# Order of loads, fills and splits at the start of a fused transformer block, and a split in two pieces at its end

## The chip, the cores and the metric

The kernel runs on one core of one Trainium2 chip. The metric is the device time of one execution in microseconds (us). Three runs of the kernel before took 1048.65, 1049.32 and 1049.63 us; their median is 1049.32 us. A core has five engines that run side by side and wait for each other through semaphores: TensorE (PE, matmuls), VectorE (DVE), ScalarE (ACT), GpSimd (POOL) and SyncE (SP), which here only issues DMAs. Each engine takes its instructions in the order in which they stand in its own queue.

## The reference

Input x has 2048 tokens of 640 features. Everything is float32.

```python
xn = layernorm(x)                                   # eps 1e-5
q, k, v = heads(xn @ wqkv)                          # 32 heads of 20
s = q @ k.T * 20 ** -0.5                            # query sees itself and the 255 tokens before it
attn = softmax(where(0 <= qi - ki < 256, s, -1e9)) @ v
mlp = (gelu(xn @ w_gate) * (xn @ w_up)) @ w_down    # 640 -> 1728 -> 640
out = x + attn @ wo + mlp
```

## The kernel before

**Precision.** A float32 operand is cut into an upper part and a lower part: ACT copies it to a tile that the matmul reads at full rate ("high", "hi"), and DVE or POOL subtracts this from the original and keeps the rest ("low", "lo"). A product is then three matmuls: high by high, low by high, high by low. So each operand costs one pass of ACT and one of DVE or POOL before PE can use it.

**Stages.** The tokens are cut into four chunks of 512 (NC = 4), each into four tiles of 128. (1) The front: the tiles are loaded, normalised and transposed, and q, k and v of the first head groups are computed. (2) Attention: a schedule of slots written out by hand interleaves scores, exponentials and sums with the projections that are still to come. (3) The gate and up products of the MLP, lines 948 and 951. (4) The last phase: the products with w_down and wo, over eight blocks of 256 tokens ("p", two to a chunk) and, in each, nine pairs of weight quads and one short step "e". For most steps (all of p of 2 and more, and the later ones of p = 1) seven products of sums stand in place of eight products, as in Strassen's scheme; a step is then 21 matmuls of 320 columns, and its operand is made of seven pieces: three taken from the loaded tile and four sums `s`.

**The first chunk** (`first_chunk`). x tiles 0 to 3 are normalised two at a time: `ln_stats` (DVE), `ln_sqrt` (DVE and ACT), `ln_rstd` (four DVE instructions), `ln_apply` (DVE, line 161: subtract the mean, scale). `turn` transposes five blocks of 128 features with PE (line 178), `high` copies the upper part from PSUM (ACT, line 349), `low` the rest (DVE, line 346), and `part` multiplies half a chunk with the weights of the first q tile (`wr0`, into `dn[0]`) and of the first k tile (`wr5`, into `dn[1]`), line 353. `high_qk` (ACT) and `low_qk` (POOL) split these weights, `load_v` splits the v weights (ACT line 298, POOL line 299) and sets up the v tiles (POOL, lines 309 and 310). `save_qk` stores q and k: ACT, DVE, ACT, POOL, then two DMAs. After it, `proj_v` makes v of the tokens of the chunk before (line 108), with the transposes of the next chunk among them: after 40 of its matmuls in chunk 1 (`VLEAD`).

**Fills.** Rows of the tiles `ks` and `qs` that hold constants are filled by 14 small DMAs on SP from a tile `ones`, which POOL sets (lines 438 and 439); POOL also builds the mask of the sliding window (lines 464 to 469).

**What sets the order.** Inside `tc.manual_schedule(engines=...)` the engines named keep the order of the program; everything else is placed by a scheduler that simulates the engines and fills each queue in the order of its own estimated times. So in the kernel before, where `first_chunk` names PE, ACT, DVE and POOL, SP is ordered by the scheduler, and work that the program writes after `first_chunk` (the v weights, the fills, the mask) is placed between its instructions. In the last phase all five engines keep the order of the program.

**The last phase** (`split_step`, `prepare`, `plan`). Step n computes its matmuls (`terms`), loads the operand of step n + 4 (SP) and splits that of step n + 2. `plan` says which weight quads are prepared at which step: `f` fetches a quad (a DMA issued by ACT), `h` makes its upper part (ACT), `l` its lower part (DVE), `s` sums, `p` single parts; `b` and `t` are the two kinds of quad. Quads pass through three staging buffers, so a fetch waits until the lower part of the quad three fetches earlier is done. `drain` adds the PSUM banks of a finished block to x and stores it.

Of the kernel before, what the change touches and what calls it, by code (L numbers as in the profile page):

```python
# [20 lines left out]
NC = S // C  # L21
# [47 lines left out]
def block_kernel(ctx, tc, x, wqk, wv, wgu, wdo, wdl, out):  # L69
# [63 lines left out]

    def ln_load(t, lp):
        xi = lp.tile([128, D], F32, name="xi", tag="xi", bufs=8)
        nc.sync.dma_start(xi, x[t * 128:(t + 1) * 128, :])
# [25 lines left out]

    def ln_scale(xs, lp, mv=None):
        n = len(xs)
        if mv is None:
            mv = lp.tile([128, n, 2], F32, name="mv4", tag="mv4", bufs=2)
            for i, xi in enumerate(xs):
                ln_stats(xi, mv[:, i, :], lp)
# [161 lines left out]
    def run(*gens):  # L330
        for gen in gens:
            for _ in gen:
                pass
# [7 lines left out]

    def first_chunk(xs, wr0, wr5, lp):
        halves = slice(0, 256), slice(256, 512)
# [4 lines left out]
        def high(k, ps, cs):  # L348
            nc.scalar.activation(xh[:, k, cs], ps, AF.Copy)
# [6 lines left out]
        def high_qk(raw):  # L356
            wh = wp.tile([128, KT, 128], F32R, name="wqh", tag="wqh")
            nc.scalar.activation(wh, raw, AF.Copy)
            return wh
# [5 lines left out]

        with tc.manual_schedule(engines=MANUAL | {mybir.EngineType.Pool}):
            mv = [lp.tile([128, 2, 2], F32, name="mv", tag="mv", bufs=2) for _ in range(2)]
# [12 lines left out]
            high(0, ta[0], halves[0])  # L380
            for k in range(1, 4):
                high(k, ta[k], halves[0])
            wh5 = high_qk(wr5)
            vb = ln_sqrt(mv[1], 2, lp)
            high(4, ta[4], halves[0])
            for k in range(2):
                low(k, ta[k], halves[0])
            rs = ln_rstd(*vb, 2, lp)
# [5 lines left out]
            nc.gpsimd.tensor_copy(one[:, 0:1], xs[3][:, 0:1])  # L394
            w5 = low_qk(wr5, wh5)
            tb = [turn(0, xs[2:4], "o")]
            for k in range(2, KT):
                low(k, ta[k], halves[0])
# [11 lines left out]
            for i, w in enumerate((w0, w5)):  # L410
                if i:
                    part(dn[i], w[1], xh, halves[0])
                part(dn[i], w[1], xh, halves[1])
                part(dn[i], w[0], xl, halves[1], last=True)
                for j in range(4 if i == 0 else 0):
                    ln_stats(xs[4 + j], mv[:, j, :], lp)
                save_qk(5 * i, 0, dn[i])
        return w0, w5, mv

    v0 = []  # L420
    with tc.tile_pool(name="lp", bufs=1, side="right") as lp:
# [11 lines left out]
        xs += [ln_load(t, lp) for t in range(4, 8)]  # L433
        w0, w5, mv1 = first_chunk(xs, wr0, wr5, lp)
        run(prep)
        v0 = v0[0]
        ones = lp.tile([4, 2 * C], BF, name="ones")
        nc.gpsimd.memset(ones, 0.0)
        nc.gpsimd.memset(ones[0:2], 1.0)
        for i in range(NK):  # L440
            for j in (0, 2):
                nc.sync.dma_start(ks[i][SR:64, j:j + 2].rearrange("p j t -> p (j t)"), ones)
        for c in range(1, NC):
            ln_scale(xs[4 * c:4 * c + 4], lp, mv1 if c == 1 else None)
            vs = [proj_v(v0, 4 * c - 4 + i, None if i % 2 else (psm, "mx")) for i in range(4)]
# [7 lines left out]
            else:  # L453
                ln_turn(4 * c, xs[4 * c:4 * c + 4])
            if c + 1 < NC:
                xs += [ln_load(t, lp) for t in range(4 * c + 4, 4 * c + 8)]
            if c == 1:
                for i in range(NQ):
                    for j in (0, 2):
                        nc.sync.dma_start(qs[i][SR + 2:64, j:j + 2].rearrange("p j t -> p (j t)"), ones[2:4])  # L460
# [683 lines left out]
    def split_step(n, between=None, behind=None):  # L1144
# [17 lines left out]
        if between:  # L1162
            between()
        sub(s[:, 0:2], raw[:, 0:1].to_broadcast([128, 2, 128]), raw[:, 1:3])
        sub(s[:, 2], s[:, 1], raw[:, 1])
        sub(s[:, 3], raw[:, 3], s[:, 2], OP.add)
        if behind:
            behind()
        nc.scalar.activation(hi[:, 3:7], s, AF.Copy)  # L1169
        sub(lo[:, 0:3], raw[:, 1:4], hi[:, 0:3].bitcast(F32))  # L1170
# [163 lines left out]
    for j, f in enumerate(range(NFA, NF - 1)):  # L1334
# [50 lines left out]
        if not end:  # L1385
# [118 lines left out]
```

## Time and profile before

| | |
|---|---|
| median of three runs | 1049.32 us |
| the profiled execution | 1047.46 us |
| its span on the core | 1045.7 us |
| PE busy | 1035.9 us, 99% |
| DVE busy | 730.8 us, 70% |
| ACT busy | 514.7 us, 49% |
| POOL busy | 333.6 us, 32% |
| granted clock of PE | 1.00 |

The times inside a profile count from the start of the span. The profiled execution is one more execution beside the three runs; what it takes beyond its span (1.76 us) lies before the first and after the last instruction. A row of the timeline gives start, length, engine, line, operation, output and inputs, shapes, how many instructions are merged into the row, and in brackets how long the engine had been idle and what ended that. Lengths of neighbouring instructions overlap a little on all engines, so the distance between starts says how fast work goes through.

### The profile page before, as it was taken

Reading aid. Unit: us, or ns where it says so; the run is one execution under the profiler, and the core shown is the slowest. Engines: PE = TensorE matmul, PEld = TensorE weight load, DVE = VectorE, ACT = ScalarE, POOL = GpSimd, SP = SyncE. Lnnn points to the kernel's source line nnn. Section 1 sums busy time; section 2 is a strip of 40 time slices with the busy share of each in tenths; the row PEclk is TensorE's granted clock in tenths of the full one; section 3 lists DMA queues with packets and bytes.
Section 4 is the critical chain, followed back from the end, with each engine's and each line's share of the span. In section 5 each row is a group of like instructions: output and inputs, shape, how many; then the busy total and the mean of one; then the engine's idle time right before and its main releaser. Section 6 shows DMA issues by size and latency. Waiting matters only on the chain.

```text
span 1045.7 us, 22718 instructions
## 1 busy us (share of the span) xinstructions
PE 1035.9 (99%) x7997; PEld 826.6 (79%) x7997; DVE 730.8 (70%) x2007; ACT 514.7 (49%) x1088; POOL 333.6 (32%) x503
## 2 busy tenths in 40 slices
PE   8999999999999999999999999999999999999998
PEld 7987666666677766666666888888888999999998
DVE  8745666666665556676663678877655889888887
ACT  4444666765665566655666522223324554333332
POOL 5121767766564458464634111110110000000000
PEclk9999999999999999999999999999999999999999
DMA  5652455545343244453322556677217874433342
GB/s 200 189 151 86 123 173 153 173 154 184 115 125 89 88 129 145 130 154 116 119 71 77 187 194 235 218 257 250 96 58 250 268 242 137 135 128 113 124 135 93
DMA packets 105179, 158.56 MB, mean 152 GB/s; under 512 B 15420, under 2 KB 60092, under 8 KB 105064
## 3 DMA queue, kind: packets, MB, share of 16 engines
q1 hardware_dynamic: 102680, 150.95, 45.0%
q10 hardware_dynamic: 2384, 6.16, 1.8%
q8 instruction: 63, 1.03, 0.4%
q14 instruction: 52, 0.43, 0.1%
HBM read 101.78 MB, written 54.92 MB: 150 GB/s over the span
## 4 chain that ended last, share of the span: by engine, by line
PE 96%; DVE 2%; DMA 1%; ACT 0%; issue 0%; SPq 0%; DVEq 0%
PE ps_d L108 23%; PE ps_g L948 21%; PE ps L1215 21%; PE ps_e L573 9%; PE ps_o L600 8%; PE ps_v L108 7%; PE ps_m L514 5%; PE ps_g L108 1%; PE ps_t L178 1%; PE ps_d L353 1%; DVE ss L1053 0%; DMA qs<-qd 0%; DVE at L1053 0%; DVE xi L161 0%; DMA xi<-x 0%
## 5 line engine op out<-in xcount | busy, mean ns | idle before, releaser
L518 DVE CUSTOM_DVE_ANT_0 junk<-ps_m,mask 128x320 bf16<-128x320 f32 (+2 forms) x512 | 243.1, 475 | 145.0 <-PE ps_m L514 87.0
L575 ACT ACTIVATE P<-ps_e 128x512 f32<-128x512 f32 (+2 forms) x384 | 198.2, 569 | 64.0 <-PE ps_e L573 58.9
L1215 PE MATMUL ps<-wb,at 128*128 128x320 f32 x999 | 156.2, 309 | 0.1
L1215 PEld LDWEIGHTS ps<-wb,at 128*128 128x128 f32 x999 | 148.9, 188 | 0.6 <-issue 0.3
L586 POOL TENSOR_SCALAR_AFFINE_SELECT P<-P 128x512 f32<-128x512 f32 x128 | 83.5, 653 | 153.6 <-ACT P L575 150.6
L573 PE MATMUL ps_e<-qs,ks 124*128 124x128 bf16 (+2 forms) x704 | 117.4, 278 | 0.3 <-ACT ob L604 0.2
L108 PE MATMUL ps_d<-xh,wqh 128*128 128x512 f32 x350 | 107.8, 416 | 0.0
L108 PE MATMUL ps_d<-xl,wqh 128*128 128x512 f32 x350 | 107.5, 415 | 0.0
L108 PE MATMUL ps_d<-xh,wql 128*128 128x512 f32 x350 | 107.2, 414 | 0.0
L1215 PE MATMUL ps<-wt,at 128*128 128x320 f32 x552 | 89.3, 310 | 0.4 <-DVE u L1053 0.4
L573 PEld LDWEIGHTS <-ks 124*128 124x128 bf16 x704 | 49.5, 98 | 47.7 <-issue 33.6
L600 PE MATMUL ps_o<-P,v 128*32 128x384 f32 (+2 forms) x1408 | 84.5, 387 | 0.0
L1215 PEld LDWEIGHTS ps<-wt,at 128*128 128x128 f32 x552 | 82.9, 188 | 0.9 <-DVE u L1053 0.9
L1169 ACT ACTIVATE at<-ss 128x512 fp32r<-128x512 f32 x59 | 37.3, 632 | 90.3 <-DVE ss L1053 90.2
L589 POOL TENSOR_SCALAR_AFFINE_SELECT P<-P 128x512 f32<-128x512 f32 x112 | 72.7, 659 | 24.8 <-ACT P L575 24.8
L101 POOL TENSOR_TENSOR wql<-wr,wqh 128x640 fp32r<-128x640 f32 x11 | 17.6, 1606 | 174.8 <-PE ps_g L948 149.5
L108 PEld LDWEIGHTS ps_d<-xh,wql 128*128 128x128 f32 x350 | 64.2, 189 | 10.4
L108 PEld LDWEIGHTS ps_d<-xl,wqh 128*128 128x128 f32 x350 | 64.2, 189 | 10.4 <-issue 0.2
L600 PEld LDWEIGHTS ps_o<-P,v 128*32 128x32 f32 x1408 | 41.4, 110 | 38.7 <-issue 21.7
L108 PEld LDWEIGHTS ps_d<-xh,wqh 128*128 128x128 f32 x350 | 63.8, 189 | 10.3 <-issue 0.2
L256 POOL TENSOR_TENSOR pt<-r,pt 128x512 bf16<-128x512 f32 x40 | 46.8, 1171 | 62.8 <-ACT pt L255 62.6
L604 ACT ACTIVATE ob<-ps_o 128x512 f32<-128x512 f32 x32 | 19.1, 597 | 88.9 <-PE ps_o L600 77.6
(194 smaller groups left out, 1849.2 us busy)
## 6 DMA issues: line engine op xcount, KB each, us to landing
hr<-hd SPq DMA_DIRECT2D x104, 128.0 KB
hd<-he SPq DMA_DIRECT2D x50, 256.0 KB
wr<-wgu SPq DMA_DIRECT2D x27, 320.0 KB
qs<-qd SPq DMA_DIRECT2D x64, 120.0 KB
ks<-kd SPq DMA_DIRECT2D x64, 120.0 KB
xi<-x SPq DMA_DIRECT2D x16, 320.0 KB
qs<-qd SPq DMA_DIRECT2D x64, 80.0 KB
ks<-kd SPq DMA_DIRECT2D x64, 80.0 KB
```

Source lines behind the costliest of these rows:

```text
L108: nc.tensor.matmul(ps, a(k), b(k), start=n == 0, stop=n == 3 * nk - 1)
L256: nc.gpsimd.tensor_tensor(out=pt[:, l, :], in0=r, in1=pt[:, 1, :], op=OP.subtract)
L514: nc.tensor.matmul(ps[64 * h:64 * h + 64, lo:hi], q[rows, j, q0:q0 + 64], keys, start=True, stop=True, tile_position=(64 * r, 64 * h))
L518: nc.vector.tensor_tensor_reduce(out=junk[:, 0:n], in0=ps[:, 0:n], in1=mask[:, 320 - n:320], scale=1.0, scalar=NEG, op0=OP.add, op1=OP.max ...
L573: nc.tensor.matmul(ps[:, col:col + n], k[0:QROWS, j, kc:kc + 128], q[0:QROWS, j, q0:q0 + n], start=True, stop=True)
L575: nc.scalar.activation(pt[:, j, lo:hi], ps[:, lo:hi], AF.Exp, scale=SCALE)
L586: nc.gpsimd.affine_select(out=a, in_=a, pattern=[[0, 4], [1, 128]], compare_op=OP.is_ge, fill=0.0, base=0, channel_multiplier=-1)
L589: nc.gpsimd.affine_select(out=a, in_=a, pattern=[[0, 4], [-1, 128]], compare_op=OP.is_ge, fill=0.0, base=-1, channel_multiplier=1)
L600: nc.tensor.matmul(o[32 * j:32 * j + 32, q0:q0 + n], v[:, w0_:w0_ + 32], pt[:, j, col:col + n], start=i == 0, stop=i == len(todo) - 1, ski ...
L948: nc.tensor.matmul(ps, i, j, start=first and n == 0, stop=n == len(work) - 1, skip_group_check=True)
L1169: nc.scalar.activation(hi[:, 3:7], s, AF.Copy)
L1215: nc.tensor.matmul(ps[bank][:, 0:HD], *work[bank][j], start=bank not in begun, stop=final[p, bank] == n and j == len(work[bank]) - 1, skip ...
```

## The change

What it does, in the order of the program:

- `ln_load` can take a tile `behind`: POOL then copies one column of that tile into the new x tile first, so that the load (which overwrites it) can't start before `behind` is there.
- `first_chunk` also keeps SP in the order of the program. All five upper parts of the first half come before the upper part of `wr5`; the square root of the second pair moves between them; one lower part instead of two stands ahead of the second pair's normalisation, and the other four behind it. The split of the v weights (`prep`) runs inside, behind that of `wr5`.
- Tiles 4 to 7 are normalised inside `first_chunk`, between the save of q and the save of k, and the loads of tiles 8 to 11 are issued there, behind tile 4's normalisation.
- The setting of `ones`, the 14 fills and the mask move behind the arrival of tile 11, into chunk 1 of the loop. The loads of tiles 12 to 15 wait until tile 8 is normalised.
- In `split_step` the upper parts of the four sums are made in two instructions of two sums, the first as soon as its sums exist.
- In `plan` three upper parts move ahead of a fetch in ACT's order.

```diff
-    def ln_load(t, lp):
+    def ln_load(t, lp, behind=None):
         xi = lp.tile([128, D], F32, name="xi", tag="xi", bufs=8)
+        if behind is not None:
+            nc.gpsimd.tensor_copy(xi[:, 0:1], behind[:, 0:1])
         nc.sync.dma_start(xi, x[t * 128:(t + 1) * 128, :])
...
-        with tc.manual_schedule(engines=MANUAL | {mybir.EngineType.Pool}):
+        with tc.manual_schedule(engines=MANUAL_OUT | MANUAL | {mybir.EngineType.Pool}):
...
             high(0, ta[0], halves[0])
-            for k in range(1, 4):
+            for k in range(1, KT):
                 high(k, ta[k], halves[0])
+            vb = ln_sqrt(mv[1], 2, lp)
             wh5 = high_qk(wr5)
-            vb = ln_sqrt(mv[1], 2, lp)
-            high(4, ta[4], halves[0])
-            for k in range(2):
-                low(k, ta[k], halves[0])
+            low(0, ta[0], halves[0])
             rs = ln_rstd(*vb, 2, lp)
...
             w5 = low_qk(wr5, wh5)
+            run(prep)
             tb = [turn(0, xs[2:4], "o")]
-            for k in range(2, KT):
+            for k in range(1, KT):
                 low(k, ta[k], halves[0])
...
                 for j in range(4 if i == 0 else 0):
                     ln_stats(xs[4 + j], mv[:, j, :], lp)
+                if i == 0:
+                    vb = ln_sqrt(mv, 4, lp)
                 save_qk(5 * i, 0, dn[i])
-        return w0, w5, mv
+                if i == 0:
+                    rs = ln_rstd(*vb, 4, lp)
+                    for j in range(4):
+                        ln_apply(xs[4 + j], mv[:, j, :], rs[:, j:j + 1])
+                    xs += [ln_load(t, lp, xs[4]) for t in range(8, 12)]
+        return w0, w5
...
-        w0, w5, mv1 = first_chunk(xs, wr0, wr5, lp)
-        run(prep)
+        w0, w5 = first_chunk(xs, wr0, wr5, lp, prep)
         v0 = v0[0]
         ones = lp.tile([4, 2 * C], BF, name="ones")
-        nc.gpsimd.memset(ones, 0.0)
-        nc.gpsimd.memset(ones[0:2], 1.0)
-        for i in range(NK):
-            for j in (0, 2):
-                nc.sync.dma_start(ks[i][SR:64, j:j + 2].rearrange("p j t -> p (j t)"), ones)
         for c in range(1, NC):
-            ln_scale(xs[4 * c:4 * c + 4], lp, mv1 if c == 1 else None)
+            if c > 1:
+                ln_scale(xs[4 * c:4 * c + 4], lp)
...
-            if c + 1 < NC:
-                xs += [ln_load(t, lp) for t in range(4 * c + 4, 4 * c + 8)]
+            if c == 2:
+                xs += [ln_load(t, lp, xs[8]) for t in range(12, 16)]
             if c == 1:
+                nc.gpsimd.tensor_copy(ones[:, 0:1], xs[11][0:4, 0:1])
+                nc.gpsimd.tensor_copy(mask[:, 0:1], xs[11][:, 0:1])
+                nc.gpsimd.memset(ones, 0.0)
+                nc.gpsimd.memset(ones[0:2], 1.0)
+                for i in range(NK):
+                    for j in (0, 2):
+                        nc.sync.dma_start(ks[i][SR:64, j:j + 2].rearrange("p j t -> p (j t)"), ones)
                 for i in range(NQ):
...
         sub(s[:, 0:2], raw[:, 0:1].to_broadcast([128, 2, 128]), raw[:, 1:3])
+        nc.scalar.activation(hi[:, 3:5], s[:, 0:2], AF.Copy)
         sub(s[:, 2], s[:, 1], raw[:, 1])
         sub(s[:, 3], raw[:, 3], s[:, 2], OP.add)
         if behind:
             behind()
-        nc.scalar.activation(hi[:, 3:7], s, AF.Copy)
+        nc.scalar.activation(hi[:, 5:7], s[:, 2:4], AF.Copy)
         sub(lo[:, 0:3], raw[:, 1:4], hi[:, 0:3].bitcast(F32))
         sub(lo[:, 3:7], s, hi[:, 3:7].bitcast(F32))
...
-            7: "ft6 ft8 hb8 lb8", 8: "ft7 ht6 lt6", 9: "ft0 ht8", 10: "lt8 ht7 lt7", 11: "ft1 ft2 ht0 lt0",
+            7: "ft6 hb8 ft8 lb8", 8: "ht6 ft7 lt6", 9: "ht8 ft0", 10: "lt8 ht7 lt7", 11: "ft1 ft2 ht0 lt0",
```

More of the change, by code (lines that the diff above doesn't have):

```diff
@@ L161, in ln_apply, with ln_scale @@
         nc.vector.tensor_scalar(xi, xi, mv[:, 0:1], rs, op0=OP.subtract, op1=OP.mult)
-    def ln_scale(xs, lp, mv=None):
+    def ln_scale(xs, lp):
         n = len(xs)
[L165 to L168, printed above, removed]
+        mv = lp.tile([128, n, 2], F32, name="mv4", tag="mv4", bufs=2)
+        for i, xi in enumerate(xs):
+            ln_stats(xi, mv[:, i, :], lp)
         rs = ln_rstd(*ln_sqrt(mv, n, lp), n, lp)
@@ L340, in block_kernel, with first_chunk @@
         nc.gpsimd.memset(nm, 0.0)
-    def first_chunk(xs, wr0, wr5, lp):
+    def first_chunk(xs, wr0, wr5, lp, prep):
         halves = slice(0, 256), slice(256, 512)
```

## The prediction, made before the changed kernel ran

> **What bounds the kernel now.** I read the page first: busy shares and the chain that ended last.
>
> ```profile
> span 1045.7 us, 22718 instructions
> PE 1035.9 (99%) x7997; PEld 826.6 (79%) x7997; DVE 730.8 (70%) x2007; ACT 514.7 (49%) x1088; POOL 333.6 (32%) x503
> PE 96%; DVE 2%; DMA 1%; ACT 0%; issue 0%; SPq 0%; DVEq 0%
> ```
>
> PE is the bound: 96% of the chain, and 9.8 us of the span in which it does nothing. The change removes no matmul. So it can win only idle PE time, and the question is where that lies. Second view: busy time by stretches (columns: from:to, length, then busy time of PE, weight loads, DVE, ACT, POOL, then granted clock, DMA share, GB/s).
>
> ```profile
> 8.00:10.00 2.00, 1.87 (x14) 1.55 (x13) 1.97 (x6) 1.36 (x5) 1.63 (x2) 1.00 0.99 401
> 10.00:12.00 2.00, 1.31 (x10) 1.11 (x10) 1.79 (x10) 1.46 (x5) 2.00 (x12) 1.00 1.03 408
> 12.00:14.00 2.00, 1.06 (x8) 0.66 (x7) 2.00 (x3) 1.38 (x4) 2.00 (x3) 1.00 0.63 245
> 30.00:62.00 32.00, 32.00 (x197) 29.51 (x196) 21.55 (x52) 13.61 (x44) 6.29 (x8) 1.00 0.52 159
> 804.00:837.00 33.00, 32.93 (x225) 32.67 (x223) 28.38 (x38) 19.44 (x25) 0.00 (x0) 1.00 0.85 284
> 880.00:900.00 20.00, 19.58 (x132) 19.08 (x131) 18.00 (x43) 9.23 (x20) 0.00 (x0) 1.00 0.37 118
> 900.00:1040.00 140.00, 140.00 (x955) 139.92 (x955) 121.41 (x282) 51.67 (x99) 0.00 (x0) 1.00 0.40 128
> 1040.00:1046.00 6.00, 2.36 (x17) 2.10 (x15) 2.00 (x5) 0.00 (x0) 0.00 (x0) 0.94 0.22 82
> ```
>
> From 8 to 14 us PE idles 0.13 + 0.69 + 0.94 = 1.76 us; the changed order of the first chunk lies there. From 880 to 900 it idles 0.42 us, where the split in two pieces works. It is full from 30 to 62 us, and in the last 140 us before the tail; the 3.64 us after 1040 are the last sums and stores, which nothing here touches. What is left lies ahead of 8 us, also untouched, and in scattered waits. The clock is full throughout the work, so it plays no part.
>
> **The first chunk.** Third view, the timeline of all engines.
>
> ```profile
> 7.08 1.14 DVE L161 TENSOR_SCALAR xi<-xi,mv,rs 128x640 f32<-128x640 f32 x2
> ...
> 8.37 0.18 POOL L375 COPY one<-xi 128x1 f32<-128x1 f32 x1 [6.51 <-DVE xi L161]
> ...
> 9.71 0.76 ACT L358 ACTIVATE wqh<-wr 128x640 fp32r<-128x640 f32 x1
> ...
> 10.34 0.32 ACT L149 ACTIVATE sq<-mv,one 128x2 f32<-128x2 f32 x1
> 10.37 0.75 DVE L346 TENSOR_TENSOR xl<-ps_t,xh 128x256 fp32r<-128x256 f32 x2
> ...
> 10.53 0.40 ACT L349 ACTIVATE xh<-ps_t 128x256 fp32r<-128x256 f32 x1
> ...
> 10.98 0.39 PE L353 MATMUL ps_d<-xh,wqh 128*128 128x256 f32 x1 [0.69 <-ACT xh L349]
> 11.03 0.15 DVE L154 RECIPROCAL rs<-sq 128x2 f32<-128x2 f32 x1
> ...
> 11.81 1.96 DVE L161 TENSOR_SCALAR xi<-xi,mv,rs 128x640 f32<-128x640 f32 x2
> 11.82 0.94 POOL L439 MEMSET ones<- 2x1024 bf16 x1
> ...
> 13.69 2.73 DVE L346 TENSOR_TENSOR xl<-ps_t,xh 128x256 fp32r<-128x256 f32 x8
> ...
> 13.82 1.20 PE L178 MATMUL ps_t<-ident,xi 128*128 128x128 f32 x9 [0.32 <-DVE xi L161]
> ...
> 14.78 1.44 PE L353 MATMUL ps_d<-xl,wqh 128*128 128x256 f32 x10
> ```
>
> *Upper parts first.* The fifth product waits 0.69 us for `high(4)`, which stands behind `wh5` (0.76 us) and the root. Changed, it starts in the place of `wh5`, 9.71, ends at 10.11, and PE goes on at about 10.17 instead of 10.98. `wh5` moves behind the root, to 10.53, and ends at 11.29; its five products are still 0.45 us earlier than before. But the gain stops there: next come the transposes of tiles 2 and 3, and these wait for DVE. So DVE's chain prices this stage.
>
> *One `low` instead of two ahead of the normalisation.* Eight take 2.73 us, so one is 0.34 us. The root is there at 10.66; the reciprocal goes from 11.03 to about 10.70, the normalisation from 11.81 to 11.48.
>
> *Fills held back.* The two normalisations took 1.96 us at 11.81, beside POOL's setting of `ones`, and 1.14 us at 7.08, with POOL empty. Changed, POOL waits for tile 3 there (its one-column copy stands ahead of the weight split, and `ones`, mask and v weights come later), so I take 1.14. DVE is through at 12.62 instead of 13.77: 0.33 + 0.82 = 1.15 us.
>
> *What is late next.* Four `low` now follow, and the transposes of blocks 1 to 4 use the PSUM banks that they free. The third of the four starts at 12.54 + 2 x 0.34 = 13.22 and ends near 13.62; then the last two transposes (nine took 0.96 to the next start, so 0.22) let the products start at 13.88 instead of 14.78. **Gain 0.90 us**, of the 1.15 and the 1.76. The ends for this part are 0 (all taken back below) and 1.76; the chain just worked out is nearer the middle, and I keep it.
>
> *Is it taken back in the same chunk?* These are the next meeting points.
>
> ```profile
> 20.35 0.64 DVE L270 TENSOR_TENSOR r<-ps_d,pt 128x512 f32<-128x512 f32 x1
> ...
> 21.73 1.17 POOL L256 TENSOR_TENSOR pt<-r,pt 128x512 bf16<-128x512 f32 x1 [1.80 <-ACT pt L255]
> 21.77 1.48 DVE L161 TENSOR_SCALAR xi<-xi,mv,rs 128x640 f32<-128x640 f32 x1
> ...
> 26.13 2.34 PE L178 MATMUL ps_t<-ident,xi 128*128 128x128 f32 x20
> ```
>
> ACT's root for tiles 4 to 7 now stands ahead of the upper part of q, so `r` starts near 20.6 although the statistics end 0.8 earlier. Its bank is wanted by the second v product, near 21.6: hidden, with 0.3 us left. The four normalisations start near 21.9, one beside POOL's 1.17 us subtraction (1.48 us, as at 21.77), three free (0.57, half of 1.14): done near 25.1, for transposes due at 26.13 - 0.90 = 25.23. Hidden, by little. A second collision costs about 0.8 there and would stall PE by 0.2 to 0.5. The save of k waits behind the four on DVE, and its store in SP behind the four loads; nothing of PE wants it before attention.
>
> **Loads, fills, mask.** The first load in the chain of waits (start, length), then SP's queue and the work that waits for it:
>
> ```profile
> 0.81 2.98 DMA xi<-x
> ```
>
> ```profile
> 12.79 5.16 SPq L442 DMA_DIRECT2D ks<-ones  x8
> 31.57 3.15 SPq L136 DMA_DIRECT2D xi<-x  x4
> 47.33 2.90 SPq L488 DMA_DIRECT2D ks<-kd  x6
> ```
>
> ```profile
> 35.82 2.18 DVE L161 TENSOR_SCALAR xi<-xi,mv,rs 128x640 f32<-128x640 f32 x4
> 38.07 2.35 PE L178 MATMUL ps_t<-ident,xi 128*128 128x128 f32 x20
> 55.88 2.35 PE L178 MATMUL ps_t<-ident,xi 128*128 128x128 f32 x20
> ```
>
> Tiles 8 to 11 go out together near 24.4 to 26.2, and no fill stands between them. PE is full from 30 to 62, so an earlier arrival gains 0; it only feeds slack. The ten added one-column copies on POOL are 0.18 us each (as the one at 8.37), 1.8 us in all, and POOL's 6.29 busy of 32 us hides them. The 14 fills (eight took 5.16 us, so 9.0) now start only after tile 11 and `ones`, by my estimate near 32, and run to about 41; the loads of tiles 12 to 15 (3.15 us) follow, issued by 44 instead of 34.7. From there it takes 10 us: landing 3.0 (first load), statistics 4 (`r` at 20.35 follows four of them, which begin when the eight `low` end at 16.4), scales 0.8 (from 11.03 to 11.81), normalising 2.2. Ready near 54, for transposes due at 55.88 - 0.90 = 55. Cost 0 while that cover holds; the first rival is its loss.
>
> **The last phase.** Groups by shape, then one ACT row and PE's timeline.
>
> ```profile
> L1053 DVE TENSOR_TENSOR at<-ss,at 128x512 fp32r<-128x512 f32 x59 | 40.8, 692 | 11.8 <-ACT at L1169 11.5
> ```
>
> ```profile
> 844.19 0.40 ACT L1150 ACTIVATE he<-hr 128x256 fp32r<-128x256 f32 x1
> ```
>
> ```profile
> 891.45 1.92 PE L1215 MATMUL ps<-wt,at 128*128 128x320 f32 x12
> ...
> 897.61 1.73 PE L1215 MATMUL ps<-wt,at 128*128 128x320 f32 x9
> 899.76 0.70 PE L1215 MATMUL ps<-wt,at 128*128 128x320 f32 x3 [0.42 <-DVE u L1053]
> ```
>
> In 59 steps DVE waits 11.5 us, about 0.2 each, for the one ACT pass over four sums. Split, the second piece covers two sums (0.40 us as 128x256) and ends while DVE makes the lower parts of the loaded pieces: the wait goes. That is worth nothing where PE is full (900 to 1040). It counts at one place: twelve matmuls take 1.92 us at 891.45, and 2.85 us from 897.61 to 899.76 + 0.70, where PE waits for DVE's sums at the change of block: 0.93 us lost. DVE is busy 18.00 of the 20 us around it, so over the four steps ahead it gains about 4 x 0.2 = 0.8 us. Ends 0 and 0.93; I take **0.85 us**, near the upper, since DVE was the late one all along. ACT pays at most one more instruction of 0.40 us a step, 24 us in 59, and it is idle for 88 of the 140 us: hidden. The reorder in `plan` frees ACT and DVE earlier in the 33 us from 804, where PE idles 0.07: 0, and it moves fetches by no more than one upper part.
>
> **The sum.** 0.90 + 0.85 = 1.75 us. The profiled execution took 1047.46 us (span 1045.7), which would become 1045.7; it lay 1.86 us below the median of the runs. Against that median: 1049.32 - 1.75 = **1047.6 us**.
>
> **Rivals.**
> *Slower: tiles 12 to 15 come too late.* The scheduler puts their loads, now behind POOL's copy and 9 us of fills, behind the q and k reloads of attention (last row of SP above, to 50.2). Then they are issued by 53.4 and ready 10 us later, at 63.4, for transposes due at 55: PE stalls 8.4 us, 1056.0. It decides from an issue later than 45. For it: SP's order there is the scheduler's, and 44 is close. Against: the loads stand ahead of the reloads in the program.
>
> *Nothing won: the held POOL work meets the next normalisation.* `ones` (0.94 us for its second half) and the mask now run just after tile 11 lands, near 30 to 34, and the four normalisations of chunk 2 (2.18 us free) follow near 34, ready near 36 for transposes due at 38.07 - 0.90 = 37.2. Each that collides costs up to 0.9 (1.48 against 2.18 / 4); three make 2.7 us, against 1 us of slack: 1.7 lost, 1049.3. For it: the rows at 11.81 and 21.77, both beside POOL. Against: the POOL work should be over by then. [...]
>
> *More won.* All 1.76 us of the first chunk and the 0.93 go, as lower parts and banks keep pace: 1049.32 - 2.69 = 1046.6.
>
> **From cases to numbers.** Within 0.2%, 2.1 us, a measurement of this kernel can't tell a change. Forecast 0.50 (of it 0.08 falls beyond 2.1 us, as the runs spread by half a us), more won 0.24, nothing won 0.16, slower 0.10. Faster 0.08 + 0.24 = 0.32; same 0.42 + 0.16 = 0.58; slower 0.10. The range runs from just below "more won", 1046.3, to 1049.9, above "nothing won"; it leaves out the slow rival.
>
> **What would show it.** Fifth product near 10.2; the pair of normalisations near 11.5 in 1.1 to 1.2 us with POOL idle; products of the lower parts near 13.9; transposes of chunk 1 near 25.2 without an idle time; DVE's wait for L1169's successors near 0 and no stretched row near 898. Wrong it would be by PE idle ahead of the transposes near 37 or 55.

## The result, and the profile after

| | before | after |
|---|---|---|
| median (22 runs of each, the same chip) | 1048.86 us | 1051.36 us |
| lowest and highest | 1047.44 and 1050.83 | 1049.62 and 1054.67 |
| ratio after to before, 95% interval | | 1.0025 [1.0017, 1.0034] |
| span of the profiled execution | 1045.7 us | 1049.0 us |

The change makes the kernel slower by 2.5 us. The forecast was 1047.6 us, no measurable change, with a range from 1046.3 to 1049.9 us. By my estimate about 1 of the 2.5 us goes with a lower mean clock of PE in nine of the 22 runs: the median of all is 1051.36 us, that of the other thirteen 1050.46 (last section).

The page of the changed kernel: its span, the busy shares, and the chain that ended last.

```profile
span 1049.0 us, 22809 instructions
PE 1037.9 (99%) x7997; PEld 827.4 (79%) x7997; DVE 732.3 (70%) x2007; ACT 524.0 (50%) x1147; POOL 336.1 (32%) x513
PE 94%; DVE 3%; DMA 1%; issue 1%; ACT 0%; POOL 0%; SPq 0%; DVEq 0%; ACTq 0%; POOLq 0%
```

The same matmuls, but PE holds 94% of the chain instead of 96%. By stretches (columns as before the change: PE's busy time is the third number):

```profile
10.00:12.00 2.00, 1.90 (x12) 1.46 (x12) 1.82 (x9) 1.84 (x6) 0.01 (x1) 1.00 1.02 406
12.00:14.00 2.00, 1.78 (x13) 1.25 (x12) 2.00 (x7) 2.00 (x7) 1.31 (x2) 1.00 1.01 399
30.00:62.00 32.00, 30.30 (x181) 27.07 (x181) 20.56 (x52) 12.15 (x41) 10.59 (x19) 1.00 0.37 114
880.00:900.00 20.00, 20.00 (x138) 20.00 (x138) 19.15 (x47) 12.18 (x31) 0.00 (x0) 1.00 0.44 132
```

The two stretches that were to win did: 0.32 us idle from 10 to 14 instead of 1.63, none from 880 to 900 instead of 0.42. The stretch that was full, 30 to 62, now has 1.70 us of idle PE.

To see where gains and losses fall, I took the start of each matmul in a trace minus the start of the same matmul in the trace of before. Negative means ahead. The median of five neighbours, in us, at these times of the kernel before (at 60 the matmuls of four kernels stand partly in another order: there it is the value of the next ones in the same order, or a blank); the rows below the first belong to the experiments.

| | 30 | 42 | 60 | 66 | 150 | 160 | 800 | 840 | 905 |
|---|---|---|---|---|---|---|---|---|---|
| the changed kernel | -0.98 | 0.03 | 1.32 | 2.83 | 2.55 | 3.96 | 4.37 | 4.23 | 3.22 |
| e1_last | 0.09 | 0.10 | 0.09 | 0.09 | 0.14 | 0.59 | 1.16 | 0.81 | -0.20 |
| e2_front | -0.78 | 0.45 | 1.74 | 5.16 | 4.87 | 6.42 | 8.02 | 7.67 | 7.64 |
| e3_order | -0.03 | -0.03 | -0.03 | -0.03 | -0.04 | 0.15 | 0.62 | 1.14 | 1.11 |
| e9_hold | 1.72 | 1.71 | 1.71 | 1.71 | 1.76 | 2.28 | 2.78 | 2.46 | 2.45 |
| e11_all | 1.15 | 1.15 | 1.15 | 1.15 | 1.17 | 1.49 | 1.51 | 1.16 | 0.15 |
| e4_x8 | 0.25 | 0.25 | 0.25 | 0.25 | -0.05 | 0.92 | 1.40 | 1.05 | 0.04 |
| e5_x12 | -0.88 | 0.45 | 0.45 | 4.99 | 5.00 | 5.41 | 5.45 | 5.10 | 4.09 |
| e6_both | 0.16 | 0.15 | 0.15 | 0.15 | -0.11 | 0.90 | 2.25 | 2.31 | 1.29 |
| e12_stats | -0.93 | 0.62 | 0.63 | 2.49 | 2.72 | 2.92 | 3.29 | 2.95 | 1.95 |
| e18_best | -0.96 | 0.36 | 0.36 | 0.38 | 0.52 | 1.37 | 1.58 | 1.23 | 0.22 |
| e19_reload | -0.86 | 0.32 | | 7.18 | 7.24 | 7.52 | 7.90 | 7.70 | 6.70 |
| e20_best2 | -0.85 | -0.64 | -0.64 | -0.64 | -0.60 | 0.41 | 0.60 | 0.25 | -0.73 |
| e21_norm2 | -0.87 | -0.87 | 0.42 | 2.76 | 2.49 | 3.17 | 3.50 | 3.47 | 2.47 |
| e22_split | -0.02 | -0.01 | -0.01 | -0.01 | 0.01 | 0.17 | 0.19 | -0.16 | -1.17 |
| e23_plan | 0.04 | 0.04 | 0.04 | 0.04 | 0.04 | -0.11 | 0.51 | 0.15 | 0.63 |

Four of these kernels (e1, e3, e22, e23) are the same as before from 66 to 800 us, and still drift by 0.2 to 1.1 us there from one execution to the next. So only the front (up to 66) and the step from 895 to 905 are read from single traces. By these, the change won 0.98 us in the first chunk, lost 1.0 at chunk 2, 1.3 at chunk 3 and 1.5 at the first scores, and won 1.0 in the last phase; 1.4 more went near 157, which is not settled (below).

The first chunk after the change, from the timeline:

```profile
9.18 1.34 PE L354 MATMUL ps_d<-xh,wqh 128*128 128x256 f32 x5
...
10.43 0.72 ACT L359 ACTIVATE wqh<-wr 128x640 fp32r<-128x640 f32 x1
...
11.42 1.14 DVE L163 TENSOR_SCALAR xi<-xi,mv,rs 128x640 f32<-128x640 f32 x2
...
12.61 1.43 PE L179 MATMUL ps_t<-ident,xi 128*128 128x128 f32 x9 [0.20 <-DVE xi L163]
...
13.80 1.44 PE L354 MATMUL ps_d<-xl,wqh 128*128 128x256 f32 x10
```

The five products run in one piece, the pair of normalisations takes 1.14 us from 11.42, and the products of the lower parts start at 13.80 (forecast: 11.48, 1.14, 13.88).

Chunk 2, the normalisation of tiles 8 to 11 (DVE), GpSimd's work, and the transposes:

```profile
33.69 0.46 POOL L476 TENSOR_SCALAR_AFFINE_SELECT mask<-mask 128x320 f32<-128x320 f32 x1
...
34.69 0.61 DVE L163 TENSOR_SCALAR xi<-xi,mv,rs 128x640 f32<-128x640 f32 x1
35.22 0.68 DVE L271 TENSOR_TENSOR r<-ps_d,pt 128x512 f32<-128x512 f32 x1
35.82 2.49 DVE L163 TENSOR_SCALAR xi<-xi,mv,rs 128x640 f32<-128x640 f32 x3
...
36.65 1.31 POOL L257 TENSOR_TENSOR pt<-r,pt 128x512 bf16<-128x512 f32 x1 [0.67 <-ACT pt L256]
37.09 0.49 PE L179 MATMUL ps_t<-ident,xi 128*128 128x128 f32 x3
38.37 2.08 PE L179 MATMUL ps_t<-ident,xi 128*128 128x128 f32 x17 [0.79 <-DVE xi L163]
```

PE comes to the transposes at 37.09, as forecast (37.2), and then waits. The mask is over by 34.15. But the subtraction `r` of chunk 1's save of q stands among the four normalisations, and it sets off GpSimd's part of that save (36.65), which runs beside the last of them. Before, the four took 2.18 us in one row and `r` came after them.

Chunk 3: SP's queue, the statistics and normalisation of tiles 12 to 15, the transposes.

```profile
33.24 5.00 SPq L466 DMA_DIRECT2D ks<-ones  x8
38.28 3.02 SPq L469 DMA_DIRECT2D qs<-ones  x5
...
43.37 1.86 SPq L138 DMA_DIRECT2D xi<-x  x4
...
48.09 0.49 DVE L143 BATCH_NORM_STATS2 st<-xi 128x6 f32<-128x320 f32 x1 [5.35 <-DMA xi<-x]
...
53.45 0.69 DVE L271 TENSOR_TENSOR r<-ps_d,pt 128x512 f32<-128x512 f32 x1 [3.48 <-ACT pt L275]
54.06 0.20 DVE L145 BATCH_NORM_AGGREGATE mv<-st 128x2 f32<-128x12 f32 x1
...
55.91 0.89 PE L108 MATMUL ps_v<-wvh,xh 128*128 128x320 f32 x5
...
57.83 3.03 DVE L163 TENSOR_SCALAR xi<-xi,mv,rs 128x640 f32<-128x640 f32 x4
...
58.46 1.52 POOL L257 TENSOR_TENSOR pt<-r,pt 128x512 bf16<-128x512 f32 x1 [2.35 <-ACT pt L256]
...
58.59 1.15 PE L179 MATMUL ps_t<-ident,xi 128*128 128x128 f32 x8 [0.17 <-DVE xi L163]
...
60.48 1.50 PE L179 MATMUL ps_t<-ident,xi 128*128 128x128 f32 x12 [0.74 <-DVE xi L163]
```

The loads are issued from 43.37 to 45.23. The first statistics start at 48.09; then `r` of chunk 2 blocks DVE for 3.48 us, and the other statistics stand behind it in the queue. The four normalisations take 3.03 us beside GpSimd's subtraction, and 2.18 us before. PE is free at 55.91, and the scheduler has put 16 products of v ahead of the transposes, 2.5 us of work that stood behind them before; so the tiles are later than the 1.3 us that PE loses. The first scores:

```profile
56.14 0.82 SPq L266 DMA_DIRECT2D qd<-pt  x2
...
60.01 0.80 SPq L266 DMA_DIRECT2D kd<-pt  x2
60.85 2.62 SPq L497 DMA_DIRECT2D ks<-kd  x6
...
65.38 0.36 PE L523 MATMUL ps_m<-ks,qs 60*64 60x64 bf16 x11 [1.21 <-DMA ks<-kd]
```

Before, the reload of k (`ks<-kd`) went out at 47.33. Now the scheduler has put it behind the stores of chunk 2's q and k, which wait for their products.

The last phase: no stretched row at the change of block, and DVE's wait for ACT (11.5 us before) is gone.

```profile
895.67 1.92 PE L1225 MATMUL ps<-wt,at 128*128 128x320 f32 x12
```

```profile
L1062 DVE TENSOR_TENSOR at<-ss,at 128x512 fp32r<-128x512 f32 x59 | 40.8, 691 | 1.4
```

### The profile page after: what moved, and what is told of

It reads as the page before. It is cut to its first block, busy times and chain, and to the rows that moved or that the text cites. A ratio compares the mean times of both kernels' runs of the same rounds, so it can differ in the third digit from the quotient of the medians.

```text
span 1049.0 us, 22809 instructions
## 1 busy us (share of the span) xinstructions
PE 1037.9 (99%) x7997; PEld 827.4 (79%) x7997; DVE 732.3 (70%) x2007; ACT 524.0 (50%) x1147; POOL 336.1 (32%) x513
## 3 DMA queue, kind: packets, MB, share of 16 engines
q1 hardware_dynamic: 102680, 150.95, 45.2%
## 4 chain that ended last, share of the span: by engine, by line
PE 94%; DVE 3%; DMA 1%; issue 1%; ACT 0%; POOL 0%; SPq 0%; DVEq 0%; ACTq 0%; POOLq 0%
PE ps L1225 23%; PE ps_d L108 22%; PE ps_g L957 21%; PE ps_e L582 9%; PE ps_o L609 8%; PE ps_v L108 5%; PE ps_m L523 5%; PE ps_g L108 1%; DMA xi<-x 1%; DVE xi L163 1%; DVE st L144 1%; DMA qs<-qd 0%; DVE st L143 0%; DVE xl L347 0%; DVE mv L145 0%
## 5 line engine op out<-in xcount | busy, mean ns | idle before, releaser
L523 PE MATMUL ps_m<-ks,qs 60*64 60x320 bf16 (+2 forms) x1472 | 61.7, 260 | 3.8 <-DVE r L271 1.3
L523 PEld LDWEIGHTS <-qs 60*64 60x64 bf16 x1472 | 27.7, 105 | 44.5 <-issue 38.8
```

Of the source, the lines that this page charges most:

```text
L523: nc.tensor.matmul(ps[64 * h:64 * h + 64, lo:hi], q[rows, j, q0:q0 + 64], keys, start=True, stop=True, tile_position=(64 * r, 64 * h))
```

## The experiments

**Theory:** both wins are real; loads, fills and a DMA order moved by the scheduler lose them again ahead of chunks 2 and 3 and of the first scores. **Rivals:** the wins aren't there; or the held GpSimd work (`ones`, mask) loses chunk 2.

### The two halves of the change apart (e1_last, e2_front)

e1: the kernel before with the edits to `split_step` and `plan` alone. e2: the changed kernel without them.

> Only the edits of the last phase, on the kernel before. Theory (the loss is all in the front, the last phase won what it could): PE's work runs as before up to 804 us and is 1.0 to 1.1 us earlier from the change of block at 899 on; time about 1.1 us under before. Rival (the extra ACT instruction per step or the moved fetches cost time somewhere): no gain at 899, or a new wait after 804, time equal to before or above.

> Only the edits of the front, on the kernel before. Theory: PE is about 1 us ahead of before from 15 to 37 us, loses 1.0 at the transposes of chunk 2, 1.4 at those of chunk 3, 1.4 at the first scores near 63 and about 1.4 near 157, and ends some 4.4 us behind: 1053.5 against 1049.3, ratio 1.004. Rival (the loss comes from both ends of the kernel together): under 3 us behind.

e1: 1047.27 us, ratio 0.9984 [0.9974, 0.9995]. e2: 1052.33, 1.0038 [1.0023, 1.0054]. From 895 to 905 e1 gains 1.0 us, e2 nothing. The loss comes with the edits of the front.

### The order and the hold, each by itself (e3_order, e9_hold)

e3 makes only the new order of the first half (the five upper parts, the root, `wh5`, one `low`). e9:

```diff
+        nc.gpsimd.tensor_copy(ones[:, 0:1], xs[3][0:4, 0:1])
+        nc.gpsimd.tensor_copy(mask[:, 0:1], xs[3][:, 0:1])
         nc.gpsimd.memset(ones, 0.0)
```

> The kernel before, with only the order of the first half changed (fifth upper part ahead of the k weights' upper part and of the root, one lower part instead of two ahead of the second normalisation); fills, mask, v weights and loads where they were. By the prediction's terms the normalisation starts 0.33 us earlier but still runs beside GpSimd (1.96 us), so the products of the lower parts start near 14.4 instead of 14.78 (0.35 us won), and nothing is late in chunks 1 to 3: 1048.4, ratio 0.9997. By a rival in which the order alone carries the whole gain, 13.9 and 0.98 us won.

> The kernel before, with only GpSimd's setting of the fill tile and the mask held until tile 3 is there (two one-column copies); no load is moved. If the collision with GpSimd is worth what the prediction says (0.82 us on the pair of normalisations), the pair at 11.81 takes near 1.14 us instead of 1.96, the transposes behind it start near 13.1, and the products of the lower parts 0.5 to 0.8 us earlier than 14.78. If something else of the change won the first chunk, nothing moves there. No wait at chunks 2 and 3, and the first scores are as before. Ratio 0.9993 to 1.0.

e3: 1.0006 [0.9997, 1.0015], and at 16 us (not in the table) it is 0.06 us ahead, where 0.35 was expected; e9 is 0.32 behind there, where it was to be 0.5 to 0.8 ahead. e9: 1.0012 [1.0002, 1.0022]. Neither wins the first chunk alone. The timeline of e9 shows why:

```profile
11.80 3.02 POOL L299 TENSOR_TENSOR wvl<-wvall,wvh 128x320 fp32r<-128x320 f32 x3 [1.03 <-ACT wvh L298]
11.85 2.24 DVE L161 TENSOR_SCALAR xi<-xi,mv,rs 128x640 f32<-128x640 f32 x2
```

With `ones` and mask held back, the lower parts of the v weights took their place beside the normalisation, which took 2.24 us instead of 1.96. In the changed kernel it is the edit that sounds least, `run(prep)` behind the split of `wr5`, that keeps GpSimd empty there (idle for 2.68 us up to 12.69, the pair runs from 11.42 to 12.56): so it follows from the order of the program, as no run has this edit alone. (In e3 the pair took 1.85 us.) e9 loses 1.4 us more in chunk 1: there the scheduler puts statistics of later tiles ahead of the normalisation of tiles 4 to 7, which takes 3.01 us from 25.04. Why it does is not shown.

### Three edits without the loads (e11_all)

The kernel before with the order of e3, the hold of e9 and the last phase.

> The kernel before with three of the edits alone: the order of the first half, the fill tile and mask held behind tile 3, and the last phase; loads, v weights and the scheduler's placing of the reloads as before. If late tiles are the loss and the rest of the change won what was forecast, it keeps 0.9 us of the first chunk and 1.0 to 1.4 us at the end: 1046.9 to 1047.3 against 1048.9, ratio 0.998. If the gain of the first chunk is taken back in chunk 1 or 2 whatever the loads do, it comes out as the last phase alone, 0.9985 to 0.999.

0.9996 [0.9985, 1.0008]. A miss: at 16 us it is 0.35 us ahead, at 30 us 1.15 behind. The v weights, still free, fill the hole as in e9, and chunk 1 loses 1.5 us, as e9 lost 1.4 there.

### Earlier loads (e4_x8, e5_x12, e6_both)

In the changed kernel, e4 issues tiles 8 to 11 without a gate ahead of the q store; e5 issues 12 to 15 ahead of the fills; e6 does both.

```diff
+            xs += [ln_load(t, lp) for t in range(8, 12)]       # e4, e6: behind the lows of tb
             mv = lp.tile([128, 4, 2], F32, name="mv4", tag="mv4", bufs=2)
...
-            if c == 2:                                          # e5, e6
-                xs += [ln_load(t, lp, xs[8]) for t in range(12, 16)]
             if c == 1:
+                xs += [ln_load(t, lp) for t in range(12, 16)]
```

> The changed kernel with the loads of tiles 8 to 11 issued at once, ahead of the store of q, and not held behind tile 4. Theory (the late tiles themselves, and the order of SP that follows from them, cost the time): statistics of tiles 8 and 9 fit ahead of the lower parts of chunk 1, the transposes of chunk 2 start near 37.1 without a wait (1.0 us won against the changed kernel); the reload of the first k tiles stands ahead of the stores of chunk 2 in SP and the first scores don't wait for it (1.4 won); the transposes of chunk 3 still come late (tiles 12 to 15 still stand behind the fills). Rival (GpSimd work beside the normalisation costs it): the transposes of chunk 2 still wait 0.8 to 1.0 us, since ones and mask are still built at the same place.

> The changed kernel with the loads of tiles 12 to 15 issued in chunk 1, ahead of the fills, and not held behind tile 8. Theory: the wait ahead of the transposes of chunk 3 goes (1.4 us won against the changed kernel), the wait at chunk 2 (1.0) and the wait of the first scores for the reload of k (1.2 to 1.4) stay. Rival (what delays chunk 3 is VectorE's queue, where the save of q of chunk 2 stands ahead of the statistics, whenever the tiles arrive): the transposes of chunk 3 wait as before the edit.

> The changed kernel, with the loads of tiles 8 to 11 ahead of the q store and those of tiles 12 to 15 ahead of the fills (both without a gate). If late tiles are the whole loss (A: chunk 2, B: chunk 3), no PE idle time stands ahead of the transposes near 37 and 55, and the k reload for the first scores comes ahead of the q store of chunk 2, so it keeps the gains of the first chunk and of the last phase except what chunk 1 loses (about 0.9 us, as with the first of these edits alone): ratio 0.9985 to 0.999. If GpSimd's held work is the cause, a wait near 37 stays.

e4: 0.9987 [0.9976, 0.9998]; no wait at chunk 2, chunk 3 or the first scores. e5: 1.0022 [1.0009, 1.0036]; chunk 3's loss is gone (0.45 at 42 and at 60), the others are not. e6: 0.9991 [0.9982, 1.0001], as e4. In e4 and e6 the gain is lost in chunk 1 instead: with the tiles there early, the scheduler puts their statistics and the mask's setting ahead of the normalisation of tiles 4 to 7. From e4's timeline, a step on 128x4 scales (0.16 us in the changed kernel at 34.49) beside GpSimd, and three normalisations of chunk 2 with nothing but one-column copies on GpSimd:

```profile
22.91 1.17 POOL L257 TENSOR_TENSOR pt<-r,pt 128x512 bf16<-128x512 f32 x1 [0.25 <-ACT pt L256]
23.07 1.02 DVE L159 SCALAR_TENSOR_TENSOR rs<-ve,rs 128x4 f32<-128x4 f32 x1
...
32.44 1.65 DVE L163 TENSOR_SCALAR xi<-xi,mv,rs 128x640 f32<-128x640 f32 x3
```

The first row ends at 24.08 and the second at 24.09: DVE's small step ends with GpSimd's instruction. So e4 and e5 bear out late tiles at chunk 3, and for chunk 2 leave open what in the new order counts.

### Order put back, then the reload (e12_stats, e18_best, e19_reload)

e12: tiles 8 and 9 early as in e4, their statistics written behind the save of k, 12 to 15 as in e5. e18: e12 with the reload written at the end of chunk 1. e19: the changed kernel with that move alone.

```diff
+            xs += [ln_load(t, lp) for t in range(8, 10)]        # e12, e18: behind the lows of tb
...
-                    xs += [ln_load(t, lp, xs[4]) for t in range(8, 12)]
+                    xs += [ln_load(t, lp, xs[4]) for t in range(10, 12)]
+            mv = lp.tile([128, 4, 2], F32, name="mv4", tag="mv4", bufs=2)
+            for j in range(2):
+                ln_stats(xs[8 + j], mv[:, j, :], lp)
...
             run(proj_qk(0, w0, c), proj_qk(5, w5, c))
+            if c == 1:                                          # e18, e19
+                load_stack(0)
...
     def attention():
-        load_stack(0)
```

> The changed kernel with the order of before put back at three places: loads of tiles 8 and 9 ahead of the q store, the statistics of 8 and 9 written behind the save of k (ahead of chunk 1's lower parts), loads of tiles 12 to 15 ahead of the fills. The k reload for the first scores still stands behind the stores of chunk 2. If late tiles and late statistics are the loss at chunks 2 and 3, neither has PE idle ahead of its transposes, and the 0.9 to 1.0 us of the first chunk lives until 60 us; the wait ahead of the first scores (1.2 to 2.7 us) stays. If work of GpSimd beside the normalisation is the cause, the wait near 37 stays at 0.8 us, since the held work lies where it lay. Ratio 0.998 to 1.001.

> As the run before this one, and the reload of the first q and k tiles is written at the end of chunk 1, so that it stands ahead of chunk 2's stores in SP's queue. If that place is what made the first scores wait, the wait near 62 to 66 goes and nothing else moves: 1.2 to 2.7 us (more with a dip of the clock) less than the run before this one, and against the kernel before the first chunk's 0.9 us and the last phase's 1.0 to 1.4 us stay: 1046.5 to 1047.0, ratio 0.998. If the wait is TensorE running ahead of DMAs whatever their order, it stays.

> The changed kernel with that one move of the reload alone. In SP's queue the 12 reloads (2.9 us for six) then stand ahead of the loads of tiles 12 to 15, so these are issued some 6 us later than 43.4 to 45.2. If the price of late tiles follows the prediction's rival (each us of issue beyond the limit is a us of PE idle time ahead of chunk 3's transposes), the wait near 58 grows from 1.4 to about 7 us: 1056 to 1058, and the first scores don't wait for the reload. If late tiles cost little and the reload's place is the loss, it comes out faster than the changed kernel.

e12: 1.0004 [0.9992, 1.0015]; e18: 0.9989 [0.9978, 1.0000]. PE's row for the first scores in e12, then in e18:

```profile
65.04 0.36 PE L529 MATMUL ps_m<-ks,qs 60*64 60x64 bf16 x11 [1.64 <-DMA ks<-kd]
```

```profile
62.92 0.36 PE L531 MATMUL ps_m<-ks,qs 60*64 60x64 bf16 x12
```

The two traces are 0.3 us apart at 60 us and 2.1 at 66. The place of the reload is the third loss, shown. But both wait 0.97 us at chunk 2, against what I expected: tiles 8 and 9 with their statistics early aren't its cure, though all four tiles early (e4, e6) are.

e19: 1.0059 [1.0038, 1.0080], 1054.18 us, where 1056 to 1058 was expected. The 12 reloads push the loads of tiles 12 to 15 to 49.65, and chunk 3's transposes wait 3.03 us (about 7 expected) and then run on a clock cut to half (granted 0.67 from 64 to 66 us and 0.50 from 66 to 68; 20 take 4.56 us, before 2.35):

```profile
49.65 2.07 SPq L138 DMA_DIRECT2D xi<-x  x4
...
63.79 4.56 PE L179 MATMUL ps_t<-ident,xi 128*128 128x128 f32 x20 [3.03 <-DVE xi L163]
```

From 42 us up to the first scores it loses 5.4 us, of these 2.2 in that row (4.56 against 2.35), which has half the clock for 3.4 us of its length (last section). It loses 1.5 more at the first scores, which now wait 1.04 us for lower parts (`xl`) and not for the reload. The changed kernel lost 1.3 at the same transposes, with an issue 6.3 us earlier. So the first rival's mechanism works, but for each microsecond of issue it costs 0.65 us, and 0.3 without the 2.2 us of that row: the scheduler has now put all 30 products of v, 4.6 us, ahead of the transposes.

### Who comes first on DVE in chunk 2 (e21_norm2, e20_best2)

e21: the changed kernel with one move; e20: e18 with the same move, and the loads of 12 to 15 behind the fills of the k tiles.

```diff
-            if c > 1:
+            if c > 2:
                 ln_scale(xs[4 * c:4 * c + 4], lp)
...
                 run(*vs)
+                if c == 1:
+                    ln_scale(xs[8:12], lp)
                 run(proj_qk(0, w0, c), proj_qk(5, w5, c))
```

> The changed kernel with one move alone: the normalisation of tiles 8 to 11 written ahead of the q and k products of chunk 1. Loads stay where the change put them. If the order on VectorE is what lost chunk 2, the wait of 0.79 us near 38 goes or falls below 0.3 us; tiles 12 to 15 are still late at a fixed time, so the wait ahead of chunk 3's transposes grows by what was saved, and the whole is no faster than the changed kernel: ratio 1.001 to 1.003. If late loads lost chunk 2, the wait near 38 stays.

> The kernel of the run with the reload moved, with two more moves: the loads of tiles 12 to 15 behind the fills of the k tiles (so that their statistics no longer come between those of tiles 8 to 11), and the normalisation of tiles 8 to 11 written ahead of the q and k products of chunk 1 (so that VectorE does all four before the save's subtraction `r`, and GpSimd's subtraction of that save comes after them). If the wait near 38 is that order, the four take near 2.2 us in one row, no PE idle time stands ahead of the transposes of chunk 2, and the 0.9 to 1.0 us of the first chunk is still there at 60 and at 150 us: with the last phase 1046.3 to 1046.8, ratio 0.9975 to 0.998. If the wait is late tiles, or the fill tile's and mask's setting, it stays at 0.8 to 1.0 us and the time is that of the run with the reload moved.

e21: 1.0019 [1.0006, 1.0032]. Its timeline:

```profile
33.93 0.45 POOL L474 TENSOR_SCALAR_AFFINE_SELECT mask<-mask 128x320 f32<-128x320 f32 x1
34.45 0.47 POOL L476 TENSOR_SCALAR_AFFINE_SELECT mask<-mask 128x320 f32<-128x320 f32 x1
...
34.97 2.18 DVE L163 TENSOR_SCALAR xi<-xi,mv,rs 128x640 f32<-128x640 f32 x4
37.06 0.68 DVE L271 TENSOR_TENSOR r<-ps_d,pt 128x512 f32<-128x512 f32 x1
...
38.49 1.16 POOL L257 TENSOR_TENSOR pt<-r,pt 128x512 bf16<-128x512 f32 x1 [1.19 <-ACT pt L256]
```

The loads are no earlier than in the changed kernel (issued from 44.12 against 43.37), the mask is set even later, and the wait is gone: -0.87 at 30 and at 42. So the order on DVE is the loss at chunk 2, shown. The rival with `ones` and mask falls. The whole gains little, as expected, but not by the way expected. Chunk 3 costs 1.3 us (-0.87 to 0.42), no more than in the changed kernel: its normalisation comes 0.90 us earlier (56.93 against 57.83) although the first statistics start later (49.12 against 48.09), and `r` comes 0.90 us earlier too (52.55 against 53.45). So in the changed kernel it is `r`, which follows PE, that sets the time of chunk 3, and not the arrival of the tiles; tiles that come ahead of `r` avoid it (e5).

The 0.9 us are lost at the first scores: 2.3 us there (0.42 to 2.76) against 1.5, with PE starting at 65.29 and 65.38, when the reload of k has landed.

e20: 0.9988 [0.9980, 0.9997], with all three losses removed; it is 0.64 us ahead from 42 to 150. Then, at the next reload of q, this row of its timeline:

```profile
157.02 0.19 PE L533 MATMUL ps_m<-ks,qs 60*64 60x64 bf16 x1 [1.07 <-DMA qs<-qd]
```

So even an undisturbed front doesn't carry its gain to the end in this execution. Before had a wait of 0.56 us at this place. Whether a DMA chain bounds every kernel there, or this is the drift of attention, stays open.

### The two edits of the last phase (e22_split, e23_plan)

Each is one of the edits of e1, on the kernel before.

> The kernel before with the upper parts of the sums in two pieces, and nothing else. By the prediction this alone wins the last phase: no stretched row near 898 (0.85 to 1.0 us), and DVE's wait for ACT in those steps near 0. The 0.36 us near 832 should not be there if the order in the plan won them. If the plan's order is what counts, the 0.93 us near 898 stay lost here. Ratio 0.999.

> The kernel before with the three upper parts ahead of the fetches in the plan, and nothing else. By the prediction 0: PE idles 0.07 us from 804 to 837, and the stretched row near 898 stays. If it is worth the 0.36 us that the run with both showed near 832, these are here alone. Ratio 0.9997 to 1.0.

e22: 0.9982 [0.9973, 0.9992]; e23: 0.9989 [0.9980, 0.9998]. e22's timeline and its group of sums, then e23's timeline:

```profile
897.44 1.92 PE L1216 MATMUL ps<-wt,at 128*128 128x320 f32 x12
```

```profile
L1053 DVE TENSOR_TENSOR at<-ss,at 128x512 fp32r<-128x512 f32 x59 | 40.8, 692 | 1.5
```

```profile
900.39 0.70 PE L1215 MATMUL ps<-wt,at 128*128 128x320 f32 x3 [0.42 <-DVE u L1053]
```

The split alone wins the 1.0 us; the plan leaves that wait where it was. The step of 0.36 us near 832 stands in both, but also in e2 and e9, which have neither edit: it most likely belongs to the trace of before. e23's trace shows no place where the plan wins (near 874 it loses 0.4 us), so I can't say where the 0.1% of its runs come from. e22 has the lowest ratio of all kernels run, but its interval overlaps those of e1, e4, e18, e20 and e23, so no best among these is shown; no version with the front is shown to do better than the last phase alone.

## Why the prediction was wrong, point by point

**First chunk, 0.90 us: right in sum and chain (0.98), but its parts don't stand alone.** Start, length and end of DVE's steps came within 0.1 us. (One small slip: 13.62 + 0.22 is 13.84, not 13.88; nothing hangs on it.) With "one `low` instead of two" alone (e3), the pair of normalisations ended 0.29 us earlier (13.48 against 13.77), near the 0.33 forecast, but the nine transposes then took 0.22 us more to the next start (1.18 against 0.96), so PE won 0.06. The prediction's chain puts this on the `low` instructions moved behind, which free the banks of the transposes, and counts it once, in its sum; no run tests it apart. And "fills held back" wins nothing while the v weights are free to move in; the term was right only because `run(prep)` moves too, which I had counted as a place and not as the price.

**"Is it taken back in the same chunk?" No: right.** Chunk 1's transposes don't wait.

**"Loads, fills, mask: cost 0": the step that failed**, by 3.8 us at three places.
- *Chunk 2 (1.0 us).* I wrote that earlier work there "only feeds slack". Its normalisation began 1.1 us earlier than before (34.69, 35.82), but the scheduler placed `r` between the normalisations, with GpSimd's subtraction behind it; why it did is not shown. `r` itself took 0.6 us of DVE. Three normalisations took 2.49 us beside the subtraction and 1.65 without it (e4): 0.84. The rival "Nothing won" named the place, the kind of collision and the price per collision, but the wrong work of GpSimd. The 1.02 us of a 128x4 instruction in e4, another kind than the normalisations, also end with GpSimd's (24.09 and 24.08). Why DVE is held up there is not shown. The one-column copies of GpSimd cost DVE nothing in e21: four of them ran from 35.71 to 37.31 beside the normalisations, which took 2.18 us as before the change.
- *Chunk 3 (1.3 us).* The issue came at 43.4 to 45.2, as estimated (44), yet "from there it takes 10 us" became 15 (45.2 to the last wait's end at 60.5). I summed the steps of the tiles and left out that DVE's queue holds `r` of chunk 2's q among them, which waits for PE: the statistics took 8.0 us instead of 4. `r` of k and one more collision with GpSimd (3.03 us against 2.18) added the rest. So the rival "Slower" decided earlier than its limit of 45, at a small price; its full price, 8.4 us for an issue by 53.4, was not reached: e19 issued by 51.7, for which the rival's rule gives 6.7 us, and lost 5.4, of them 2.2 in the row at half the clock.
- *First scores (1.5 us).* "Nothing of PE wants it before attention" was said of k's store; that the reloads could fall behind the stores of chunk 2 was not seen. The change doesn't touch their code: the scheduler gave them another place when the work around them moved.

**Last phase, 0.85 us: right (1.0), and by the split, as said. Plan 0: right as far as a trace can tell.**

**"The clock is full throughout the work, so it plays no part": right for the two profiled executions (mean clock 1.000 and 0.999), not for all runs.** Waits like those that the change brings were followed by half the clock for 3.4 us in three traces, and nine of the changed kernel's 22 runs have a mean clock as low as those, 0.998 (last section).

The sum forecast -1.75; the trace has -2.0 for the same two terms, +3.8 for the one set to 0, and +1.4 near 157 whose cause is open. "Wrong it would be by PE idle ahead of the transposes near 37 or 55": both came.

## What to carry to other kernels

Where a scheduler fills the queues, an edit in one stage also moves DMAs and single instructions that it doesn't name; print the order of every queue before and after, and look for late-waiting instructions (a store, a subtraction on a fresh PSUM bank) that have come ahead of something due. A gain early in a pipeline counts only if the next arrival that doesn't move with it (here a reload) isn't later than the new due time: e21 saved a microsecond at 38 us and lost it at the first scores, 25 us on. Holding work back to free an engine doesn't free it while other work may move into the hole.

## What the runs showed that I had not expected

In three traces a wait of PE is followed by half the clock for 3.4 us. In e5 PE waits 0.88 and then 1.80 us for the reload; timeline, then stretches:

```profile
65.95 0.35 PE L522 MATMUL ps_m<-ks,qs 60*64 60x64 bf16 x11 [1.80 <-DMA ks<-kd]
...
67.84 2.33 PE L108 MATMUL ps_d<-xh,wql 128*128 128x512 f32 x5
```

```profile
66.00:68.00 2.00, 2.00 (x17) 1.58 (x18) 1.32 (x7) 0.00 (x0) 0.00 (x0) 0.77 0.63 180
68.00:70.00 2.00, 2.00 (x7) 1.52 (x6) 0.14 (x2) 0.00 (x0) 0.00 (x0) 0.50 0.64 195
70.00:72.00 2.00, 2.00 (x15) 1.25 (x13) 0.00 (x0) 0.38 (x1) 0.00 (x0) 0.88 0.68 199
```

The granted clock (third number from the end) falls to half, by these numbers for (0.23 + 0.50 + 0.12) x 2 us / 0.5 = 3.4 us. The 15 products from 66.24 take 5.13 us up to the next one's start (71.37), and the same 15 took 3.53 in the kernel before (62.85 to 66.38): 1.6 us on top of the wait. It also stands in e2 behind a wait of 1.38 us (clock 0.70, 0.50 and 0.94 in the stretches from 66 to 72) and in e19 behind one of 3.03 us (0.67, 0.50 and 0.98 from 64 to 70), by the same sum for 3.4 us each. In e21 a wait of 1.89 us at the same place had no such dip, and in the trace of the changed kernel 1.21 us had none (both have 1.00 in every stretch from 62 to 72), so the length of one wait doesn't decide it. What does is not shown.

A mean clock as low as with this dip goes with the upper half of the changed kernel's spread. Over all 17 traces the mean granted clock of the execution is 0.998 in these three (e2, e5, e19), and 0.999 or 1.000 in the others. Of the changed kernel's 22 runs nine show 0.998 and took 1051.92 to 1054.67 us, with a median of 1053.33; the other thirteen have a median of 1050.46, which is 1.6 us above the kernel before, and not 2.5. Of the 129 runs of the kernel before that were made beside the experiments, 15 show 0.998. Whether these runs have such a dip, and where, is not recorded.
